# First inverse units behind the final spectral products, other loads held back, and 1/std in the transposes of the first layernorm

## The chip, the cores and the metric

The kernel runs on one core of one Trainium2 chip. Its engines work side by side: TensorE (PE in the profile, its weight loads PEld) multiplies matrices, VectorE (DVE), ScalarE (ACT) and GpSimd (POOL) work element by element, SyncE (SP) issues most transfers. Transfers run on 16 DMA engines. The metric is the device time of one execution in microseconds (us); less is better.

## What is computed

A conditioned block: a layernorm with scale and shift, a long convolution whose kernel comes from a diagonal state-space model, a gated residual, a second layernorm, a gated feed-forward part, a second residual. Sequence 2048, width 640, 128 states for each channel, hidden width 1728, all in float32.

```python
    mod = (_silu(c) @ w_mod).reshape(c.shape[0], 6, 1, -1)
    sa, ca, ga, sb, cb, gb = ...
    h = _layernorm(x, axis=-1) * (1 + ca) + sa
    x = x + ga * _A_ref(h, ...)      # S4D: K = 2 Re(C exp(A dt t)); y = irfft(rfft(u) rfft(K)) + u D
    h = _layernorm(x, axis=-1) * (1 + cb) + sb
    x = x + gb * _B_ref(h, ...)      # (silu(h w1) * (h w3)) w2
```

## The kernel before

**Two stages.** In the first, the convolution is computed for five groups of 128 channels (b = 0 to 4): the kernel's samples are generated, kernel and input go through a two-step Fourier transform on PE, the spectra are multiplied on DVE, and an inverse first step gives `zt`, which is stored to the DRAM buffer `zd`. In the second, the feed-forward part runs over four blocks of 512 rows (b = 0 to 3), each with 14 tiles of the hidden width (`ORDER`: 0, 13, 1 to 12; tile 13 is 64 wide, its gate and up halves in one matmul).

**The order of stage one** is made by a planner (`Plan`). Each task has an engine, an estimated cost, predecessors, buffers that it takes and gives, and a rank from a fixed table (`RANKS`). The planner simulates the tasks, and issues them in the order that comes out. `InOrder` fixes that order on every engine. A DMA task has a list of sizes from which the planner estimates its landing. So a changed predecessor or size may change the order of what comes after it.

**The final spectra** (`spectra_tasks` with b = 4). There are eight units i. For each, PE makes the spectrum of the input (`w4.i.f`, in the profile `fh`) and of the kernel (`w4.i.k`, `fk`), ACT holds the first (`w4.i.h`, `hz`), DVE multiplies in three steps (`w4.i.x0`, `x1`, `c`, `fp`). Every second unit completes a pair j, for which PE makes the inverse first step (`z4.j.z`, `fz`, 8 matmuls), two evictions follow (`z4.j.v0`, `v1`, into `zt`, three buffers), and two stores (`z4.j.o0`, `o1`, in the profile `zd<-zt`; the very last is `zd<-ztl` or `zd<-zt`). The planner's lines all carry the source line L157, that of the wrapper.

**Inverse units.** The second step of the inverse transform works on units of two row groups j: it loads a part of `zd` (`inverse_load`, 4 DMAs, `iz`), multiplies it with the constant `wd` on PE (`inverse`, `iy`), and DVE adds the result to the rows `x2`. Block 0 of the feed-forward part needs units 0 and 1. Their first 512 channels (groups 0 to 3 of stage one) are done inside the plan: tasks `iz0`, `iz1` (loads) and `ir0`, `ir1` (matmuls, additions, and the statistics `bn_stats` of these channels). The last 128 channels need the last stores; they are loaded behind the plan as `izb`, half from SP's queue and half from ACT's, and added in `self.inverse(0, 4, z, ps, ...)`. The last of these matmuls is `self.hold`: every DMA issued with `held_back` waits for it. Around them stand `awake` matmuls without a result. Units 2 to 7 run inside block 0 of the feed-forward part, in `mid`.

**The task `change`** closes the buffers of stage one and opens those of the feed-forward part. It loads `x2` of block 0 (4 DMAs) and `wd` (1 MB). `fw0` and `fw1` load the weights of the first two tiles of block 0 (`wr`, `w2r`), which ACT and POOL split into a high and a low part (`wh`, `wl`, `w2h`, `w2l`), as every operand of the feed-forward part is. All these transfers stand on SP's queue, which issues in order; the planner reckons with at most eight in flight.

**Layernorm of a block** (`ln2`): `bn_stats` per 128 channels, `bn_aggr` per row group, `rsqrt` (13 small operations on 128x4: an integer estimate and three Newton steps, then -mean/std), the normalised rows `xn` on ACT and DVE, PE transposes with the identity (`tp`), scale and shift by `cols` into `v`, and the split into `xh` and `xl`. For block 0 the 5 transposed tiles use the banks of `acc`.

**Feed-forward.** `up` makes gate and up (`gu`, three matmuls for each of 5 parts and each half: high by high, low by high, high by low); for the first two tiles of block 0 it runs jointly, part by part. `gate` makes `th`, `a`, `ah`, `al`; `down` adds to `acc`. The weights of a tile are asked for with `weights`, at the tile; their buffers are two deep. From `at(1000)` on, order is made by the framework's scheduler: program order by priority, where operands are ready. Its simulation lets a transfer go as soon as its buffer is free.

```python
        nxt = {0: self.ln2(0, pool, ps, self.stats, po)}
        self.at(2000)
        self.load_x2(1)

        def mid(b, m):
            if b == 0 and m in (1, 3):
                self.load_x2((m + 3) // 2)
            if b == 0 and 2 <= m + 1 < 8:
                self.inverse_unit(m + 1, ip, ps, "gu", 3)
```

Of the kernel before, what the change touches and what calls it, by code (L numbers as in the profile page):

```python
# [282 lines left out]
class K:  # L283
# [385 lines left out]
    def ln2(self, b, pool, ps, stats=None, po=None):  # L669

        nc = self.nc
        xs = self.x2[b]
        st, mv = stats or self.ln_begin(pool, f"n{b}")
        for j in range(4):
            self.ln_part(st, xs, j, KT - 1 if stats else 0, KT)
        rstd, nb = self.ln_end(pool, st, mv, f"n{b}")
        xn = pool.tile([P, 4, D], F32, name=f"xn{b}", tag="xn", bufs=1)
        for j in range(4):
            if j % 2:
                nc.vector.tensor_scalar(xn[:, j, :], xs[:, j, :], rstd[:, j:j + 1], nb[:, j:j + 1], op0=ALU.mult, op1=ALU.add)  # L680
            else:
                nc.scalar.activation(xn[:, j, :], xs[:, j, :], AF.Identity, scale=rstd[:, j:j + 1], bias=nb[:, j:j + 1])
        xh = pool.tile([P, KT, 512], F32R, name=f"xh{b}", tag="xh", bufs=2)
        xl = pool.tile([P, KT, 512], F32R, name=f"xl{b}", tag="xl", bufs=2)
        for k in range(KT):
            if po:
                pt = po.tile([P, 512], F32, name=f"tp{b}{k}", tag=f"acc{k}")
            else:
                pt = ps.tile([P, 512], F32, name=f"tp{b}{k}", tag="gu", bufs=3)
            for j in range(4):  # L690
                nc.tensor.transpose(pt[:, j * P:(j + 1) * P], xn[:, j, k * P:(k + 1) * P], self.ident)
# [11 lines left out]
    def weights_load(self, b, m, wp, ahead=False):  # L703

        nc = self.nc
        two = m < 13
        n = 2 if two else 1
        dma = (nc.gpsimd if ahead and POOLQ else nc.sync).dma_start
        raw = wp.tile([P, 2, KT, P], F32, name=f"wr{b}_{m}", tag="wr", bufs=2)
        f0 = m * P  # L710
        for i, src in enumerate((self.w1, self.w3)):
            if two:
                dma(raw[:, i], src[:, f0:f0 + P].rearrange("(k p) f -> p k f", p=P))
            else:
                dma(raw[:, 0, :, i * 64:(i + 1) * 64], src[:, f0:].rearrange("(k p) f -> p k f", p=P))
        w2r = wp.tile([P, D], F32, name=f"w2r{b}_{m}", tag="w2r", bufs=2)
        if two:
            dma(w2r, self.w2[m * P:(m + 1) * P, :])
        else:
            for i in range(2):  # L720
                dma(w2r[i * 64:(i + 1) * 64], self.w2[1664:1728, :])

        parts = []

        def high():
            wh = wp.tile([P, 2, KT, P], F32R, name=f"wh{b}_{m}", tag="wh", bufs=2)[:, :n]
            w2h = wp.tile([P, D], F32R, name=f"w2h{b}_{m}", tag="w2h", bufs=2)
            if b == 3:

                nc.vector.tensor_mul(w2r[:, :512], w2r[:, :512], self.gb)  # L730
            for i in range(n):
                self.nc.scalar.activation(wh[:, i], raw[:, i], AF.Copy)  # L732
# [22 lines left out]
    def ffn(self, nxt, wp, pool, ps, po, mid):  # L755

        pend = None
        for b in range(4):
            acc = None
            for i in range(14):  # L760
                m = self.ORDER[i]
                if b == 0 and i < 2:
                    if i == 0:
                        w = [self.ahead.pop((0, x)) for x in range(2)]
                        both = self.up(0, [(self.ORDER[x], *w[x][:2]) for x in range(2)], *nxt[0], ps)
                    w2h, w2l = w[i][2:]
                    gu = both[i]
                else:
                    wh, wl, w2h, w2l = self.ahead.pop((b, i), None) or self.weights(b, m, wp)
                    gu, = self.up(b, [(m, wh, wl)], *nxt[b], ps)  # L770
                if pend is not None:
                    self.down(*pend)
                    if i == 0:
                        self.output(b - 1, pend[1], pool, ps)
                if acc is None:
                    acc = [po.tile([P, 512], F32, name=f"acc{b}{k}", tag=f"acc{k}") for k in range(KT)]
                ah, al = self.gate(b, m, gu, pool)
                pend = (m, acc, ah, al, w2h, w2l)
# [79 lines left out]
    def run(self):  # L858
# [48 lines left out]
        def change():  # L907
            close("gw", "tbl", "gp", "early")
            self.xp, self.ip, self.wp = open_("xp"), open_("ip"), open_("wp")
            self.wd = self.xp.tile([P, NJ, 2, 64], F32, name="wd")  # L910
            self.x2 = [self.xp.tile([P, 4, D], F32, name="x20")]
            nc.sync.behind = nc.tensor.prev
            self.load_x2(0)
            nc.sync.dma_start(self.wd, self.t_wd)
            nc.sync.behind = None
            self.stats = self.ln_begin(self.ip, "n0")
        add = plan.add
        add("change", None, 0, change, [f"g{b}.7.p", f"g{b}.7.d"] + [f"h{b}.{i}.x" for i in range(4)], 0)
        add("fx", "SP", 0, None, ["change"], 0, dma=[327680] * 4 + [1048576])
        self.ahead = {}  # L920
        split = {}
        cut = b * P
# [5 lines left out]
            add(f"fs{m}", "POOL", 5.0, lambda m=m: self.ahead.__setitem__((0, m), split[m][1](self.nc.gpsimd)), [f"fa{m}"], W + 30)  # L928

        def load_w(m):  # L930
            q = nc.gpsimd if POOLQ else nc.sync
# [9 lines left out]
            for j in (2 * u, 2 * u + 1):  # L941
                self.ln_part(self.stats[0], self.x2[0], j, 0, KT - 1)
        for u in range(2):
            add(f"iz{u}", "SP", 0, lambda u=u: load_z(u), ["change", "fx"] + [f"z{b - 1}.{j}.o{f}" for j in range(4) for f in range(2)], W, dma=[262144] * 4)
            add(f"ir{u}", "PE", 2.4, lambda u=u: first_rows(u), [f"iz{u}"] + [f"{x}{b}.{i}.e" for x in ("hh", "k") for i in range(8)], W + 25)
        plan.run()
        self.nc = real
        self.at(1000)
# [5 lines left out]
        ps = open_("ps", space=PSUM)  # L954
        self.x2 += [pool.tile([P, 4, D], F32, name=f"x2{b}") for b in range(1, 4)]
        z = self.inverse_load("izb", ip, "izb", 1, 0, 4, cut, D, real.scalar)
        self.awake(nc.tensor, po.tile([P, 512], F32, name="awake0", tag="acc4"), 8)
        self.hold = nc.tensor.prev = self.inverse(0, 4, z, ps, "gu", 3, cut, D)
        self.awake(nc.tensor, po.tile([P, 512], F32, name="awake1", tag="acc4"), 3)
        nxt = {0: self.ln2(0, pool, ps, self.stats, po)}  # L960
        self.at(2000)
        self.load_x2(1)

        def mid(b, m):
            if b == 0 and m in (1, 3):
                self.load_x2((m + 3) // 2)
            if b == 0 and 2 <= m + 1 < 8:
                self.inverse_unit(m + 1, ip, ps, "gu", 3)
            if b == 0 and m == 9:
                self.gb_row(pool, ps)  # L970
            if m == 8 and b < 3:
# [385 lines left out]
    def early_tasks(self, e):  # L1357
# [133 lines left out]
        add("cols", "ACT", .9, lambda: self.mod_cols(pm[1]), ["mc4"], W["col"], take=[("f2", 1), ("hz", 1)])  # L1491
        add("colsf", None, 0, None, ["cols"], give=[("f2", "cols"), ("hz", "cols")])

    def gb_row(self, pool, ps):

        pr = ps.tile([P, 512], F32, name="prg", tag="gu", bufs=3)
# [64 lines left out]
```

## Time and profile before

| | |
|---|---|
| runs | 998.25 us median of 3 (996.02 to 1000.65) |
| the profiled execution | 998.14 us, span from first to last instruction 996.4 us |
| granted TensorE clock, mean | 0.975 |
| PE busy | 893.9 us, 90% of the span |
| DVE / ACT / POOL busy | 665.9 / 496.8 / 287.7 us |
| DMA | 122.03 MB, mean 122 GB/s |
| stage one | up to about 384 us |
| feed-forward part | first up matmul at 398.52 us, to the end |

A page of the profile and the queries of its trace give: windows (busy time of each engine in a stretch), the chain of waits (the work that ended last, followed back from step to step), the timeline (instructions in order of time: start, length, engine, line, operation, output and inputs, count, and in brackets the idle time before and what ended it), groups (instructions of one line and shape: busy us, mean ns), DMA issues (sizes, and time from issue to landing). Lengths of PE instructions overlap: the time of a row of matmuls is read from start to start.

### The profile page before, as it was taken

Reading aid. Unit: us, or ns where it says so; the run is one execution under the profiler, and the core shown is the slowest. Engines: PE = TensorE matmul, PEld = TensorE weight load, DVE = VectorE, ACT = ScalarE, POOL = GpSimd, SP = SyncE. Lnnn points to the kernel's source line nnn. Section 1 sums busy time; section 2 is a strip of 40 time slices with the busy share of each in tenths; the row PEclk is TensorE's granted clock in tenths of the full one; section 3 lists DMA queues with packets and bytes.
Section 4 is the critical chain, followed back from the end, with each engine's and each line's share of the span. In section 5 each row is a group of like instructions: output and inputs, shape, how many; then the busy total and the mean of one; then the engine's idle time right before and its main releaser. Section 6 shows DMA issues by size and latency. Waiting matters only on the chain.

```text
span 996.4 us, 20192 instructions
## 1 busy us (share of the span) xinstructions
PE 893.9 (90%) x8095; PEld 708.2 (71%) x8095; DVE 665.9 (67%) x1234; ACT 496.8 (50%) x829; POOL 287.7 (29%) x293
## 2 busy tenths in 40 slices
PE   1464777889999997999999999999999999999997
PEld 1133666767788863667788888888888888888885
DVE  7998999999999674677564553463644544645443
ACT  6878787979788731432243332342432332433221
POOL 1798798989898330100000000000000000000000
PEclk9986998999999999999999999999999999999999
DMA  9955553615041297997232363332443323542301
GB/s 215 266 177 188 123 132 99 156 45 129 24 108 46 73 266 206 221 236 173 61 98 73 106 166 92 86 100 79 118 134 107 92 80 94 145 119 80 106 27 53
DMA packets 141189, 122.03 MB, mean 122 GB/s; under 512 B 13480, under 2 KB 124840, under 8 KB 139688
## 3 DMA queue, kind: packets, MB, share of 16 engines
q1 hardware_dynamic: 140360, 119.84, 45.6%
q8 instruction: 63, 1.03, 0.5%
q10 hardware_dynamic: 736, 0.92, 0.3%
q14 instruction: 30, 0.25, 0.1%
HBM read 99.75 MB, written 20.97 MB: 121 GB/s over the span
## 4 chain that ended last, share of the span: by engine, by line
PE 72%; DVE 13%; DMA 5%; ACT 4%; issue 3%; POOL 1%; SPq 1%; ACTq 0%; DVEq 0%; POOLq 0%
PE acc L833 19%; PE gu L798 13%; PE gu L797 12%; PE gu L796 12%; PE ps L157 4%; DVE yy L157 3%; DMA xs<-in_x 3%; PE kps L157 2%; PE fk L157 2%; PE fz L157 2%; DVE fp L157 2%; DMA zd<-zt 2%; PE fh L157 2%; DVE hn L157 2%; DVE xx L157 2%
## 5 line engine op out<-in xcount | busy, mean ns | idle before, releaser
L798 PE MATMUL gu<-xh,wl 128*128 128x512 f32 x540 | 213.1, 395 | 0.0
L797 PE MATMUL gu<-xl,wh 128*128 128x512 f32 x540 | 211.8, 392 | 0.0
L796 PE MATMUL gu<-xh,wh 128*128 128x512 f32 x540 | 210.7, 392 | 0.7 <-ACT xh L666 0.7
L732 ACT ACTIVATE wh<-wr 128x640 fp32r<-128x640 f32 x105 | 71.9, 732 | 135.6 <-PE gu L797 129.3
L744 POOL MEMSET w2l<- 64x640 f32 x3 | 1.9, 630 | 451.0 <-PE acc L833 451.0
L797 PEld LDWEIGHTS gu<-xl,wh 128*128 128x128 f32 x540 | 101.6, 188 | 23.6 <-DVE xl L667 0.2
L796 PEld LDWEIGHTS gu<-xh,wh 128*128 128x128 f32 x540 | 101.4, 188 | 23.2 <-ACT xh L666 1.0
L798 PEld LDWEIGHTS gu<-xh,wl 128*128 128x128 f32 x540 | 101.6, 188 | 21.3
L809 ACT ACTIVATE th<-gu 128x512 f32<-128x512 f32 x52 | 31.1, 598 | 127.7 <-PE gu L798 127.5
L811 DVE TENSOR_TENSOR a<-a,gu 128x512 f32<-128x512 f32 x52 | 35.8, 688 | 86.2 <-PE gu L798 85.9
L157 POOL TENSOR_TENSOR yy<-e,e 128x512 f32<-128x512 f32 x80 | 86.3, 1094 | 17.9 <-PE kps L157 11.8
L833 PE MATMUL acc<-w2h,ah 128*128 128x512 f32 x220 | 87.1, 396 | 0.0
L833 PE MATMUL acc<-w2l,ah 128*128 128x512 f32 x220 | 87.1, 396 | 0.0
L733 ACT ACTIVATE w2h<-w2r 128x640 fp32r<-128x640 f32 x54 | 39.9, 738 | 94.6 <-issue 53.0
L810 DVE SCALAR_TENSOR_TENSOR a<-th,gu 128x512 f32<-128x512 f32 x52 | 35.7, 687 | 76.1 <-ACT th L809 76.0
L745 DVE TENSOR_TENSOR w2l<-w2r,w2h 128x640 fp32r<-128x640 f32 (+1 forms) x54 | 44.4, 822 | 58.0 <-ACT w2h L733 57.9
L741 DVE TENSOR_TENSOR wl<-wr,wh 128x640 fp32r<-128x640 f32 x105 | 82.4, 819 | 0.0
L157 POOL TENSOR_TENSOR ph<-p,p 128x1024 int32<-128x1024 int32 x40 | 79.9, 1997 | 5.2 <-ACT tr L157 4.5
L833 PE MATMUL acc<-w2h,al 128*128 128x512 f32 x204 | 77.6, 396 | 0.0
L157 DVE TENSOR_TENSOR yy<-yy,tr 128x512 f32<-128x512 f32 (+1 forms) x80 | 75.5, 946 | 0.9 <-ACT tr L157 0.6
L157 PE MATMUL kps<-yy,xx 128*32 128x64 f32 x2560 | 52.7, 239 | 24.9 <-DVE xx L157 21.9
L157 PEld LDWEIGHTS kps<-yy,xx 128*32 128x32 f32 x2560 | 46.1, 119 | 34.5 <-issue 17.5
(231 smaller groups left out, 1694.7 us busy)
## 6 DMA issues: line engine op xcount, KB each, us to landing
wr<-in_w SPq DMA_DIRECT2D x104, 320.0 KB, 3.9
w2r<-in_w SPq DMA_DIRECT2D x52, 320.0 KB, 3.0
zd<-zt SPq DMA_DIRECT2D x39, 256.0 KB, 2.7
iz<-zd SPq DMA_DIRECT2D x24, 320.0 KB, 9.2
xs<-in_x SPq DMA_DIRECT2D x16, 320.0 KB, 11.2
hs<-hb SPq DMA_DIRECT2D x20, 256.0 KB, 2.4
xb<-hs SPq DMA_DIRECT2D x20, 256.0 KB, 4.5
x<-in_x SPq DMA_DIRECT2D x16, 320.0 KB, 9.8
```

The lines of the kernel that those rows point to most:

```text
L157: self.prev = self.k.order(f(*a, **kw), self.prev)
L732: self.nc.scalar.activation(wh[:, i], raw[:, i], AF.Copy)
L733: self.nc.scalar.activation(w2h, w2r, AF.Copy)
L741: eng.tensor_tensor(wl[:, i], raw[:, i], wh[:, i].bitcast(F32), op=ALU.subtract)
L745: eng.tensor_tensor(w2l[q], w2r[q], w2h[q].bitcast(F32), op=ALU.subtract)
L796: nc.tensor.matmul(pg, wh[:, k, :], xh[:, k, :], start=(k == 0), stop=False)
L797: nc.tensor.matmul(pg, wh[:, k, :], xl[:, k, :], start=False, stop=False)
L798: nc.tensor.matmul(pg, wl[:, k, :], xh[:, k, :], start=False, stop=(k == KT - 1))
L809: nc.scalar.activation(th, gu[0], AF.Tanh, scale=0.5)
L810: nc.vector.scalar_tensor_tensor(a, th, 1.0, gu[0], op0=ALU.add, op1=ALU.mult)
L811: nc.vector.tensor_mul(a, a, gu[1])
L833: nc.tensor.matmul(acc[k], *two(a, w), start=(m == 0 and i == 0), stop=(m == 12 and i == 2))
```

## The change

1. **Units 0 and 1 in the plan.** `iz{u}` (the loads) now also follow the evictions `z4.u.v0`, `z4.u.v1`. `ir{u}` (the matmuls, additions and statistics) now also follow `z4.3.z`, the last `fz`. The sizes by which the planner estimates the loads become two of 512 KB in place of four of 256 KB; the DMAs themselves are the same four.
2. **`wd`.** `change` loads only the first quarter of it (256 KB); the rest is loaded with `held_back`, behind `x2` of block 1.
3. **Weights.** All loads of `weights_load` go by `held_back`. The two that are issued inside the plan are not touched, since `hold` isn't set there. The third tile's are issued once after the layernorm of block 0, ahead of `x2` of block 1; the fourth's and later ones at their tiles, as before in program order, but not before `hold`.
4. **Units 2 to 7** run in `mid` of tile u instead of u - 1.
5. **`awake`** ahead of the `izb` products: 3 calls in place of 8.
6. **Layernorm of block 0.** `xn` becomes mean - x, on ACT for all four row groups, each behind its own `bn_aggr`. `rsqrt_short` has 9 small operations. Four DVE operations make diagonals `dg` from the identity and the result. The 20 transposes become 20 f32 matmuls with `xn` stationary and `dg` moving, so that the transposed rows come out scaled by 1/std. Blocks 1 to 3 keep `ln_end` and the transposes.

```diff
+        if po:
+            dg = pool.tile([P, 4, P], F32, name="dg", bufs=1)
+            for j in range(4):
+                nc.vector.bn_aggr(mv[:, j, :], st[:, j, :, :])
+                nc.scalar.activation(xn[:, j, :], xs[:, j, :], AF.Identity, scale=-1.0, bias=mv[:, j, 0:1])
+            y = self.rsqrt_short(pool, mv[:, :, 1], 4)
+            for j in range(4):
+                nc.vector.tensor_scalar(dg[:, j, :], self.ident, y[:, j:j + 1], -0.375, op0=ALU.mult, op1=ALU.mult)
...
-                nc.tensor.transpose(pt[:, j * P:(j + 1) * P], xn[:, j, k * P:(k + 1) * P], self.ident)
+                if po:
+                    nc.tensor.matmul(pt[:, j * P:(j + 1) * P], xn[:, j, k * P:(k + 1) * P], dg[:, j, :], start=True, stop=True)
+                else:
+                    nc.tensor.transpose(pt[:, j * P:(j + 1) * P], xn[:, j, k * P:(k + 1) * P], self.ident)
...
-        dma = (nc.gpsimd if ahead and POOLQ else nc.sync).dma_start
+        def dma(to, src):
+            self.held_back(nc.sync.dma_start(to, src))
...
-                    wh, wl, w2h, w2l = self.ahead.pop((b, i), None) or self.weights(b, m, wp)
+                    wh, wl, w2h, w2l = self.third() if (b, i) == (0, 2) else self.weights(b, m, wp)
...
-            nc.sync.dma_start(self.wd, self.t_wd)
+            nc.sync.dma_start(self.wd[:, :4], self.t_wd[:, :4])
...
-        add("fx", "SP", 0, None, ["change"], 0, dma=[327680] * 4 + [1048576])
+        add("fx", "SP", 0, None, ["change"], 0, dma=[327680] * 4 + [262144])
...
-            add(f"iz{u}", "SP", 0, lambda u=u: load_z(u), ["change", "fx"] + [f"z{b - 1}.{j}.o{f}" for j in range(4) for f in range(2)], W, dma=[262144] * 4)
-            add(f"ir{u}", "PE", 2.4, lambda u=u: first_rows(u), [f"iz{u}"] + [f"{x}{b}.{i}.e" for x in ("hh", "k") for i in range(8)], W + 25)
+            add(f"iz{u}", "SP", 0, lambda u=u: load_z(u), ["change", "fx"] + [f"z{b - 1}.{j}.o{f}" for j in range(4) for f in range(2)] + [f"z{b}.{u}.v{f}" for f in range(2)], W, dma=[524288] * 2)
+            add(f"ir{u}", "PE", 2.4, lambda u=u: first_rows(u), [f"iz{u}", f"z{b}.3.z"] + [f"{x}{b}.{i}.e" for x in ("hh", "k") for i in range(8)], W + 25)
...
-        self.awake(nc.tensor, po.tile([P, 512], F32, name="awake0", tag="acc4"), 8)
+        self.awake(nc.tensor, po.tile([P, 512], F32, name="awake0", tag="acc4"), 3)
...
         self.at(2000)
+        self.third = self.weights_load(0, self.ORDER[2], wp)
         self.load_x2(1)
+        self.held_back(nc.sync.dma_start(self.wd[:, 4:], self.t_wd[:, 4:]))
...
-            if b == 0 and 2 <= m + 1 < 8:
-                self.inverse_unit(m + 1, ip, ps, "gu", 3)
+            if b == 0 and 2 <= m < 8:
+                self.inverse_unit(m, ip, ps, "gu", 3)
...
+    def rsqrt_short(self, pool, var, n):
+        V = self.nc.vector
+        v, w, h, q = (pool.tile([P, n], F32, name=f"rq_{x}", bufs=1) for x in "vwhq")
+        V.tensor_scalar(v, var, 1.0, EPS, op0=ALU.mult, op1=ALU.add)
+        V.tensor_scalar(w.bitcast(I32), v.bitcast(I32), -0.5, float(0x5F3759DF), op0=ALU.mult, op1=ALU.add)
+        V.tensor_mul(h, v, w)
+        V.scalar_tensor_tensor(h, h, -0.5, w, op0=ALU.mult, op1=ALU.mult)
+        V.scalar_tensor_tensor(w, h, 1.5, w, op0=ALU.add, op1=ALU.mult)
+        V.tensor_mul(h, v, w)
+        V.tensor_mul(h, h, w)
+        V.scalar_tensor_tensor(q, h, -10.0 / 3, h, op0=ALU.add, op1=ALU.mult)
+        V.scalar_tensor_tensor(q, q, 5.0, w, op0=ALU.add, op1=ALU.mult)
+        return q
```

More of the change, by code (lines that the diff above doesn't have):

```diff
@@ L675, in ln2 @@
             self.ln_part(st, xs, j, KT - 1 if stats else 0, KT)
-        rstd, nb = self.ln_end(pool, st, mv, f"n{b}")
+        dg = None
         xn = pool.tile([P, 4, D], F32, name=f"xn{b}", tag="xn", bufs=1)
[L678 to L682, printed above, removed]
+        if po:
[7 more added lines that the diff above has]
+        else:
+            rstd, nb = self.ln_end(pool, st, mv, f"n{b}")
+            for j in range(4):
+                if j % 2:
+                    nc.vector.tensor_scalar(xn[:, j, :], xs[:, j, :], rstd[:, j:j + 1], nb[:, j:j + 1], op0=ALU.mult, op1=ALU.add)
+                else:
+                    nc.scalar.activation(xn[:, j, :], xs[:, j, :], AF.Identity, scale=rstd[:, j:j + 1], bias=nb[:, j:j + 1])
         xh = pool.tile([P, KT, 512], F32R, name=f"xh{b}", tag="xh", bufs=2)
@@ L690, in ln2 @@
             for j in range(4):
-                nc.tensor.transpose(pt[:, j * P:(j + 1) * P], xn[:, j, k * P:(k + 1) * P], self.ident)
+                if po:
+                    nc.tensor.matmul(pt[:, j * P:(j + 1) * P], xn[:, j, k * P:(k + 1) * P], dg[:, j, :], start=True, stop=True)
+                else:
+                    nc.tensor.transpose(pt[:, j * P:(j + 1) * P], xn[:, j, k * P:(k + 1) * P], self.ident)
             v = pool.tile([P, 512], F32, name=f"v{b}{k}", tag="v", bufs=3)
@@ L930, in load_w @@
         def load_w(m):
-            q = nc.gpsimd if POOLQ else nc.sync
+            q = nc.sync
             q.behind = nc.tensor.prev
```

## The prediction

> **What bounds the kernel now.** I looked first at the page for the busy shares, then at the stretch where the convolution hands over to the feed-forward part: the windows, the chain of waits, the timeline of each engine, the DMA queue. Columns of the windows: stretch, length, busy us and instructions of PE, PEld, DVE, ACT and POOL, then granted clock, DMA share, GB/s.
>
> ```profile
> 345.00:384.10 39.10, 36.65 (x360) 24.42 (x357) 23.79 (x55) 13.03 (x22) 8.24 (x6) 0.96 1.01 261
> 363.57:366.98 3.41, 1.36 (x14) 0.57 (x10) 2.94 (x7) 1.67 (x3) 3.37 (x3) 1.00 1.10 275
> 366.98:370.40 3.42, 3.35 (x11) 1.66 (x11) 0.69 (x1) 0.60 (x1) 2.16 (x2) 0.50 1.10 290
> 392.00:450.00 58.00, 53.81 (x248) 38.09 (x247) 40.32 (x107) 22.90 (x34) 2.59 (x2) 1.00 1.04 227
> ```
>
> From 345 to 384 and again from 392 to 450 the DMA engines are full. In the window at 363.6 PE sits idle for 2 us, and in the next it runs at half clock. The chain of waits (start, length, what) through this place:
>
> ```profile
> 363.66 6.04 DMA zd<-zt
> 369.76 8.34 DMA zd<-zt
> 378.19 0.61 ACT zt L157
> 378.81 5.28 DMA zd<-zt
> 384.11 0.67 ACTq L642
> 384.81 3.81 DMA izb<-zd
> 391.39 0.30 DVE mv_n L350
> 394.41 0.93 ACT xn L682
> 395.38 1.76 PE tp L691 x14
> 398.52 0.97 PE gu L796 x3
> ...
> 543.75 3.49 PE acc L833 x15
> ```
>
> So between 363.7 and 384.1 the end is set by stores of `zd`, each slow because the queue is full, and by the buffers `zt` that these stores give back. Behind the last store come its reload `izb`, the layernorm, and the first up matmul at 398.52. After that PE sets the pace (the last row: 15 matmuls back to back, 0.23 us each).
>
> **The seam: inverse units moved, loads held.** PE and DVE there, by the timeline:
>
> ```profile
> 363.13 1.07 PE L157 MATMUL fk<-sp,wb 128*64 128x128 f32 x16
> 364.51 0.68 DVE L157 TENSOR_TENSOR fp<-fk,hz 128x512 f32<-128x512 f32 x1
> 365.83 0.75 DVE L157 TENSOR_TENSOR fp<-fp,fk 128x256 f32<-128x256 f32 x2
> 366.25 4.09 PE L157 MATMUL iy<-iz,wd 128*64 128x512 f32 x7 [2.05 <-DMA iz<-zd]
> 374.94 2.29 PE L157 MATMUL fz<-fp,wz 64*128 64x512 f32 x8 [0.34 <-DVE fp L157]
> 377.15 1.94 PE L157 MATMUL iy<-iz,wd 128*64 128x512 f32 x8
> 379.56 6.60 PE L157 MATMUL awake<-wd,ident 128*128 128x512 f32 x15
> ```
>
> Unit 0 (`iy` at 366.25) stands in PE's order ahead of the last spectral unit. It waits 2.05 us for its load and blocks PE for 4.09 more; the last `fh` and `fk` come behind it, and the last `fz` only at 374.94. With both units behind the last `fz`, unit 7's `fh` and `fk` follow the `fk` that ends at 364.20: 2 x 1.07 gives 366.34. DVE needs 2.07 us a unit (364.51 to 366.58), and ends this one at 368.7. The last `fz` then runs from 368.9 for 2.29 us to 371.2 instead of 377.2, its last eviction (0.61) ends at 371.8, and the last store is issued at 371.9 instead of 378.81. If the `fz` of pair 2 slips in between, this is up to 2.3 us later, which the longest flight below stands for.
>
> The store's flight: the loads that filled the queue are gone.
>
> ```profile
> 367.48 1.09 SPq L713 DMA_DIRECT2D wr<-in_w  x2
> 370.83 4.42 SPq L713 DMA_DIRECT2D wr<-in_w  x2
> 375.34 0.84 SPq L718 DMA_DIRECT2D w2r<-in_w  x1
> wd<-in_t_wd SPq DMA_DIRECT2D x1, 1024.0 KB, 10.1
> DMA to landing us min/median/max: 2.3/4.0/5.6
> ```
>
> The last row is the flight of the `zt` stores, 2.3 to 5.6 us. I take 3.3, under the median, since only unit 1's load is still draining. The last store lands at 371.9 + 3.3 = 375.2 instead of 384.09 (378.81 + 5.28): **8.9 us** earlier; by the bounds 6.6 (5.6 us flight) to 9.9 (2.3 us). The queue must be able to follow: six weight loads of 327,680 bytes (1.97 MB) and three quarters of `wd` (0.79 MB) leave this stretch, 2.75 MB, at 261 GB/s 10.5 us. So the queue allows the same, and neither bound undercuts the other. On SP the two loads of 4 DMAs each now stand behind the first stores of pairs 0 and 1, which lets `zt` go earlier; the later stores stand behind the loads, whose data land before PE reaches the units at 371.2.
>
> What must stay covered: units 0 and 1 now run at the very end, 2 x 1.94 us of PE, to 375.1. Their DVE work is 4 additions and 16 statistics:
>
> ```profile
> L157 DVE TENSOR_TENSOR x<-iy,x 128x512 f32<-128x512 f32 x4 | 2.8, 692 | 6.3 <-PE iy L157 6.2
> L157 DVE BATCH_NORM_STATS2 st_n<-x 128x6 f32<-128x128 f32 x16 | 3.3, 278 | 0.0
> ```
>
> 6.1 us, from 371.8 to 377.9, hidden by the last store's flight and the reload, which (4.5 us from issue to landing, 384.11 to 388.62) ends at 379.7. Cover gone, as with a load of unit 1 that lands 2 us later than I have it, each further us counts in full. The keep-awake matmuls take 0.44 us each, two to a call: 3 calls end at 377.7; 8 would have ended at 382.1, on the path. PE then idles some 2 us. The rows above show half clock after a window busy for 1.36 of 3.41 us; the same here would cost up to 1.7 us. The Trainium skill (TensorE: Matmul & The Clock Gate, What's actually happening) has the clock fall only after at least one idle window of about 3.4 us; here 2 us of idle were enough, so the measurement decides, and by the page alone this cost would be nothing.
>
> **Layernorm of the first block.**
>
> ```profile
> 390.62 0.58 DVE L350 BATCH_NORM_AGGREGATE mv_n<-st_n 128x2 f32<-128x30 f32 x3
> 391.77 0.17 DVE L325 TENSOR_SCALAR rs_v_n<-mv_n 128x4 f32<-128x4 f32 x1
> 394.15 0.16 DVE L337 SCALAR_TENSOR_TENSOR rs_n_n<-mv_n,rs_y_n 128x4 f32<-128x4 f32 x1
> 394.41 1.73 ACT L682 ACTIVATE xn<-x,rs_n_n,rs_y_n 128x640 f32<-128x640 f32 x2 [15.63 <-DVE rs_n_n L337]
> 395.30:397.90 2.60, 2.40 (x20) 2.17 (x20) 1.00 1.04 221
> 514.90:516.20 1.30, 1.05 (x8) 1.00 (x8) 1.00 0.00 0
> ```
>
> Call A the end of the last aggregate, 391.69. Before: 13 small operations, 0.2 us apart (391.77 to 394.15), `xn`, first transpose at A+3.7, 20 of them in 2.4 us, first up matmul at A+6.8. After: 9 small operations take 1.8 us, to A+1.9; four diagonals of 128x128 (no such operation here; between the 0.17 us of the 128x4 row and the 0.28 us of the 128x128 statistics, I take 0.2, nearest in size) are there from A+2.1 to A+2.7. The four centred `xn` on ACT (1.73 for two, so 0.82 apart) start behind the first aggregate, about 391.0, and end at A+2.7: hidden by the diagonals. PE starts at A+2.15 and no longer transposes but multiplies. The last two rows are PE's 20 transposes, and the four plain f32 products of the same 128x128 shape of `gb_row`, which stand as 8 records: 1.05 us / 8 = 0.13 a record with its tail, 0.11 without. Twenty products are 40 records, 4.5 us, so PE is through at A+6.7 and the first up matmul, whose `xh` is long ready, follows there: **-0.1 us**. Bounds: -0.6 (0.11 a record, no wait for the fourth `xn`) to +1.0 (0.13 and a late fourth).
>
> The Trainium skill (TensorE: Matmul & The Clock Gate, Terms) calls the transpose mode "4× faster for FP32"; the rows make it 2.2 (0.26 for two records against 0.12).
>
> **What the held loads cost later.** All 2.75 MB now wait for the last `izb` product, at 390.03 - 8.9 = 381.1, where SP starts the next loads.
>
> ```profile
> 390.03 3.79 SPq L632 DMA_DIRECT2D x<-in_x  x8
> 393.86 11.31 SPq L642 DMA_DIRECT2D iz<-zd  x8
> 411.97 10.59 SPq L713 DMA_DIRECT2D wr<-in_w  x4
> 408.31 2.62 ACT L732 ACTIVATE wh<-wr 128x640 fp32r<-128x640 f32 x4
> 412.73 2.59 PE acc L833 x10
> ```
>
> In the order of the program stand the weights of the third tile (0.98 MB), `x2` of block 1 (1.31), the rest of `wd` (0.79), `x2` of block 2 (1.31), unit 2 (1.31), the weights of the fourth tile (0.98): 6.7 MB, at 227 GB/s 29.4 us and 2 us to the first byte, landed at 412.5. Up to here PE has, from 389.5, the joint up product of 45 matmuls (at 0.23 us, 10.3), a gap of about 2.4 for `th` to `ah` (3.9 before, from 398.52 + 10.3 to 412.73, partly filled with unit 2, which now comes a tile later), `down` 3.5, up 6.9, the narrow `down` 2.3: the fourth tile is due at 414.9. That is just enough. The fifth stands behind 3.6 MB more, 428.4, and is due at 427.7; from there each tile moves 2.3 MB, 10.1 us, against 12.8 of PE. I charge **+1.0 us**. Bounds: -1.3 (two `wh` conversions instead of four stand ahead of `ah` on ACT, 2.62 / 2) to +5 (a tenth less bandwidth over 10.3 MB).
>
> **The sum** is made against the profiled execution, 998.14 us (its span of 996.4 and 1.7 around it), 0.1 us under the median 998.25 of the runs: 998.14 - 8.9 - 0.1 + 1.0 = **990.1 us**. Its own range: the good bounds together, -9.9, -0.6 and -1.3, give 986.3; -6.6 with +1.0 and +3 of the loads 995.5.
>
> **Rivals.**
> 1. *Starved first block, slower.* If SP issues as it did (8 `x`, 8 `iz`, more `x`, then `wr` at 411.97), `x2` of block 3 and unit 3 (2.6 MB, 11.5 us) get ahead of the fourth tile's weights: landed at 424, PE waits 10.7 us, and the idle window halves the clock, 1.7: 998.14 - 8.9 - 0.1 + 1.0 + 10.7 + 1.7 = 1002.5. For it: the saturated windows, and that the rows show `wr` last. Against it: those were later tiles; the fourth tile's stand ahead in the program. It decides once those weights land more than 9 us after 414.9.
> 2. *The order on SP keeps the stores back.* The change does only half of what it says: stores of pairs 2 and 3 sit behind the load of unit 1 in a queue still full, the last one leaves 3 us later and flies 5.6: 998.14 - 3.9 - 0.1 + 1.0 = 995.1. For it: 1.01 DMA share; against it: 2.75 MB less.
> 3. *Dear products.* Four times a transpose, 20 x 0.12 x 4 = 9.6 us, puts the first up matmul at A+11.75, 4.9 us later than now: 998.14 - 8.9 + 4.9 + 1.0 = 995.1. The `gb_row` record speaks against it. This is the factor of the skill's page named above.
>
> **The chances.** The forecast 0.75, starved 0.12, stores 0.08, products 0.05. A difference under 0.5% (5 us, faster under 993.3, slower over 1003.2) can't be told from none. Of the forecast 0.70 lies below 993.3 and 0.05 above; rivals 2 and 3 are no change; of the starved case 0.05 is no change and 0.07 slower. Faster 0.70, same 0.23, slower 0.07. The range 986.5 to 996.0 holds the forecast but its edge (0.04) and rivals 2 and 3; it leaves out the starved case.
>
> **What would show it.** The last `fz` ends near 371 with the clock at 1.00 throughout, the last `zd` store lands at 375 (right) or past 379 (rival 2); `iy` of both units follows; aggregates to first up matmul 6.7 us, PE's 40 records about 4.5 (rival 3: 9.6); PE without waits for `wr` in the first block, `wh` of the fourth tile near 411 (rival 1: near 424). If DVE still works on the units' statistics when `izb` lands, or blocks 1 to 3 are not as long as before, the reasoning is wrong.

## The result and the profile after

The changed kernel takes **1011.91 us** (median of 4 runs, 1011.55 to 1013.72), the kernel before, run beside it, 997.70 us (4 runs, 996.02 to 1000.65). The ratio is 1.0137, with a 95% interval of 1.0120 to 1.0154: **slower**, by 1.4%. The prediction was 990.1 us, with 996.0 as its upper end. It was wrong.

The profiled execution took 1011.79 us, its span is 1010.0. Three marks divide the span: the first up matmul, the first transpose of block 1, and the end.

| stretch, us | before | after | difference |
|---|---|---|---|
| start to the first up matmul | 398.52 | 391.32 | -7.2 |
| block 0, up to the first transpose of block 1 | 103.99 | 118.13 | +14.1 |
| blocks 1 to 3 and the end | 493.9 | 500.5 | +6.7 |
| span | 996.4 | 1010.0 | +13.6 |

So the seam gave about what it should, and two later places took back three times as much. PE, SP and DVE at the seam, by the timeline of the changed kernel (start, length, engine, line, what, count, idle before):

```profile
367.66 4.73 PE L157 MATMUL fz<-fp,wz 64*128 64x512 f32 x16
372.32 3.65 PE L157 MATMUL iy<-iz,wd 128*64 128x512 f32 x16
377.78 2.84 PE L157 MATMUL awake<-wd,ident 128*128 128x512 f32 x6 [1.81 <-DVE x L157]
373.58 0.42 SPq L157 DMA_DIRECT2D zd<-zt  x1
376.87 1.25 SPq L642 DMA_DIRECT2D izb<-zd  x2
384.02 0.29 DVE L682 BATCH_NORM_AGGREGATE mv_n<-st_n 128x2 f32<-128x30 f32 x1
386.13 0.87 DVE L686 TENSOR_SCALAR dg<-ident,rq_q 128x128 f32<-128x128 f32 x4
386.57 4.70 PE L703 MATMUL tp<-dg,xn 128*128 128x128 f32 x40 [1.17 <-DVE dg L686]
391.32 0.97 PE L811 MATMUL gu<-xh,wh 128*128 128x512 f32 x3
```

The last `fz` ends at 372.4 (377.2 before), the last store leaves at 373.58 (378.81) and its reload at 376.87 (384.1). The 40 records of the new products take 4.70 us. The chain of waits (start, length, what) goes another way here than through the reload:

```profile
376.54 1.20 DVE x L157 x2
377.78 2.84 PE awake L157 x6
380.62 2.02 PE iy L652 x16
```

The `awake` matmuls waited 1.81 us for the additions of the two units on DVE, and the products of the reload start right behind them. The reload left from 376.87 to 377.6 and was 2.9 to 3.6 us on its way, so its data came between 379.7 and 381.1, about when `awake` was through.

Then the first block. ACT's timeline, PE's one row where it stops and the row where it goes on, and the chain of waits (start, length, what):

```profile
400.78 0.60 ACT L824 ACTIVATE th<-gu 128x512 f32<-128x512 f32 x1 [4.14 <-PE gu L813]
401.30 1.37 ACT L747 ACTIVATE wh<-wr 128x640 fp32r<-128x640 f32 x2
411.88 0.74 ACT L747 ACTIVATE wh<-wr 128x640 fp32r<-128x640 f32 x1 [9.21 <-DMA wr<-in_w]
412.64 0.59 ACT L830 ACTIVATE th<-gu 64x512 f32<-64x512 f32 x1
...
414.07 0.74 ACT L747 ACTIVATE wh<-wr 128x640 fp32r<-128x640 f32 x1 [0.36 <-DMA wr<-in_w]
414.71 0.61 ACT L666 ACTIVATE ah<-a 128x512 fp32r<-128x512 f32 x1
...
427.89 1.42 ACT L747 ACTIVATE wh<-wr 128x640 fp32r<-128x640 f32 x2 [9.58 <-DMA wr<-in_w]
429.21 0.61 ACT L666 ACTIVATE ah<-a 128x512 fp32r<-128x512 f32 x1
```

```profile
409.38 0.40 PE L813 MATMUL gu<-xh,wl 128*128 128x512 f32 x1
415.38 0.80 PE L848 MATMUL acc<-ah,w2h 128*128 128x512 f32 x1 [5.60 <-ACT ah L666]
```

```profile
387.38 13.45 DMA x<-in_x
400.85 13.20 DMA wr<-in_w
417.50 10.02 DMA wr<-in_w
430.51 2.40 PE acc L848 x5
```

In ACT's queue the conversions `wh` of the fourth tile stand ahead of `ah` of the first tile. They wait 9.21 us for `wr`, and `ah`, whose input `a` was done on DVE at 403.5, waits behind them. PE's first `down` needs this `ah`: PE is through with all up products that it can do at 409.8 and idles 5.60 us. With the fifth tile it happens again, 9.58 us on ACT and, by the trace's starts and ends, 4.7 on PE.

Before, `ah` stood behind four conversions too, but these had their weights, and it came 13.5 us after the first up matmul (398.52):

```profile
412.05 0.63 ACT L666 ACTIVATE ah<-a 128x512 fp32r<-128x512 f32 x1
```

After the change, on SP, `x2` of block 2 and the load of unit 2 left ahead of the fourth tile's weights:

```profile
386.76 4.42 SPq L632 DMA_DIRECT2D x<-in_x  x4
392.26 6.51 SPq L642 DMA_DIRECT2D iz<-zd  x4
399.51 1.73 SPq L723 DMA_DIRECT2D wr<-in_w  x2
```

What idle time does to the clock, by windows (stretch, length, busy us of PE, PEld, DVE, ACT, POOL, clock, DMA share, GB/s):

```profile
391.32:509.45 118.13, 107.77 (x466) 76.83 (x467) 69.48 (x189) 33.42 (x52) 2.58 (x2) 0.96 0.71 171
410.16:413.58 3.42, 0.00 (x0) 0.00 (x0) 0.83 (x1) 1.68 (x3) 0.00 (x0) 1.00 1.12 254
413.58:416.99 3.41, 1.61 (x4) 1.32 (x5) 2.81 (x4) 1.87 (x4) 0.00 (x0) 0.50 0.99 205
416.99:420.41 3.42, 3.42 (x10) 2.65 (x9) 2.06 (x3) 1.25 (x2) 0.00 (x0) 0.50 1.00 237
423.82:427.24 3.42, 2.03 (x10) 0.95 (x8) 0.00 (x0) 0.00 (x0) 0.00 (x0) 1.00 0.95 230
427.24:430.65 3.41, 0.14 (x1) 0.14 (x2) 1.99 (x4) 2.76 (x5) 0.00 (x0) 1.00 0.25 74
430.65:434.06 3.41, 3.41 (x9) 1.54 (x9) 3.41 (x10) 0.43 (x1) 0.00 (x0) 0.50 0.80 207
```

Three windows of 3.41 us run at half clock; PE is busy in 8.4 us of them, and half of that, 4.2, is lost. Before, the same block had its PE busy for 103.16 of 103.99 us, at full clock:

```profile
398.52:502.51 103.99, 103.16 (x466) 74.83 (x467) 70.96 (x191) 34.27 (x53) 2.59 (x2) 1.00 0.74 170
```

Blocks 1 to 3 have no waits in either kernel. There the chain shows one row for each tile's `down`, so the distance of two rows is the period of a tile (30 up and 15 down matmuls). Before, then after:

```profile
533.38 3.49 PE acc L833 x15
543.75 3.49 PE acc L833 x15
```

```profile
540.76 3.50 PE acc L848 x15
551.29 3.50 PE acc L848 x15
```

10.37 us became 10.53 (551.29 - 540.76). The 39 full tiles of these blocks by 0.16 give 6.2 of the 6.7 us. From start to start, by the trace, neighbouring up matmuls stand 234.4 ns apart in place of 229.9, the down matmuls 234.1 in place of 232.7 (means; how long a gap still counts as back to back moves them all by up to 0.5 ns). The code there is the same.

### The profile page after: what moved, and what is told of

Read it like the earlier page. It is cut to its first block, busy times and chain, and to the rows that moved or that the text cites. A ratio compares the mean times of both kernels' runs of the same rounds, so it can differ in the third digit from the quotient of the medians.

```text
span 1010.0 us, 20218 instructions
## 1 busy us (share of the span) xinstructions
PE 901.1 (89%) x8105; PEld 710.5 (70%) x8105; DVE 666.3 (66%) x1233; ACT 497.2 (49%) x830; POOL 286.7 (28%) x293
## 4 chain that ended last, share of the span: by engine, by line
PE 72%; DVE 14%; DMA 5%; ACT 4%; issue 3%; SPq 1%; POOL 1%; DVEq 0%; ACTq 0%
PE acc L848 18%; PE gu L811 12%; PE gu L813 12%; PE gu L812 12%; PE ps L157 4%; DVE yy L157 3%; PE fz L157 3%; PE fk L157 2%; PE kps L157 2%; DMA wr<-in_w 2%; PE fh L157 2%; DVE fp L157 2%; DVE xx L157 2%; PE iy L652 2%; DVE hn L157 1%
## 5 line engine op out<-in xcount | busy, mean ns | idle before, releaser
L811 PE MATMUL gu<-xh,wh 128*128 128x512 f32 x540 | 214.2, 398 | 0.1
```

What stands on the lines that cost most here:

```text
L811: nc.tensor.matmul(pg, wh[:, k, :], xh[:, k, :], start=(k == 0), stop=False)
```

## The experiments

Two theories were to be tested, with their rivals. **Queue**: in block 0, late weights hold up conversions, and what stands behind these holds up PE; the rival is bandwidth alone. **Place**: the small tiles `rs_*` of `ln_end` used to be allocated by block 0, ahead of `xh`; now block 1 allocates them, behind it. So `xh`, `xl`, `v`, `th`, `a`, `ah`, `al` and `u` begin 160 bytes lower (`xh` at 154944 in place of 155104 in each partition), and matmuls that read from there are slower; the rival is that the later start or the other order does it.

The remainder is that of the start of `xh` by 512 bytes; the two paces are means from start to start in blocks 1 to 3. Idle PE is the length of block 0 less PE's busy time in it. Runs of one group shared their chip and the runs of the kernel before; the other columns are from one profiled execution of each kernel.

| kernel | remainder | up, down ns | block 0 us | idle PE there | us, ratio to before, interval |
|---|---|---|---|---|---|
| before | 480 | 229.9, 232.7 | 104.0 | 0.8 | |
| after | 320 | 234.4, 234.1 | 118.1 | 10.4 | 1011.91, 1.0137 (1.0120 to 1.0154) |
| e1_shift | 288 | 233.0, 232.2 | 121.5 | 14.0 | 1009.34, 1.0110 (1.0084 to 1.0137) |
| e2_before_shift | 448 | 233.6, 233.2 | 104.4 | 0.8 | 1003.44, 1.0051 (1.0020 to 1.0082) |
| e3_order | 320 | 234.4, 234.1 | 114.4 | 8.8 | 1008.21, 1.0104 (1.0077 to 1.0130) |
| e4_early | 320 | 234.4, 234.1 | 109.1 | 3.9 | 1009.49, 1.0122 (1.0096 to 1.0149) |
| e5_place | 480 | 230.4, 232.7 | 117.3 | 10.4 | 1005.06, 1.0069 (1.0044 to 1.0094) |
| e6_spread | 320 | 234.4, 234.1 | 105.9* | 6.9 | 1007.59, 1.0086 (1.0060 to 1.0111) |
| e7_both | 480 | 230.4, 232.7 | 105.6* | 7.7 | 1001.10, 1.0021 (1.0004 to 1.0038) |
| e8_place_x | 480 | 229.6, 233.0 | 117.7 | 11.3 | 1004.28, 1.0062 (1.0041 to 1.0083) |
| e9_all | 480 | 230.5, 232.7 | 95.5* | 0.1 | 992.03, 0.9930 (0.9914 to 0.9946) |
| e10_x2_late | 480 | 230.4, 232.7 | 103.9 | 1.3 | 990.22, 0.9918 (0.9896 to 0.9940) |
| e11_ln | 480 | 230.5, 232.8 | 107.8 | 3.0 | 998.45, 0.9996 (0.9983 to 1.0010) |
| e12_x512 | 0 | 233.7, 233.4 | 105.2 | 1.3 | 996.10, 0.9970 (0.9957 to 0.9982) |

(*: here some units stand behind the first transpose of block 1, which makes block 0 shorter and what follows longer.)

### The place of the tiles

**e1_shift and e2_before_shift**: 32 bytes of padding, in the changed kernel and in the one before.

```diff
-        u = pool.tile([P, 512], F32, name=f"u{b}", tag="u", bufs=1)
+        u = pool.tile([P, 520], F32, name=f"u{b}", tag="u", bufs=1)[:, :512]
```

> The changed kernel with one tile made 32 bytes longer, so that every tile of the feed-forward pool that lies before it, xh and xl among them, starts 32 bytes lower. In the kernel before they start at 32 beyond a multiple of 64 bytes, in the changed one on a multiple. Theory placement: the 1620 up matmuls of the changed kernel stand 0.234 us apart instead of 0.230 because of where their moving operand starts; the shift brings 0.230 back and 7 us of time, 1005 us. Rival: the slower pace has another cause (transfers, the clock); 1012 us, 0.234.

> The kernel before with the same 32 bytes, so that xh and xl come to lie on a multiple of 64. Theory placement: 0.234 us and 7 us slower, 1005 us. Rival: 998 us, 0.230.

In the kernel before, the padding alone, with the order of work unchanged, moves the up matmuls from 229.9 to 233.6 ns and makes the kernel 0.5% slower (1.0051): a place costs some 5 us by itself. A tile's period, by the chain:

```profile
535.53 3.50 PE acc L833 x15
546.02 3.50 PE acc L833 x15
```

That is 10.49 us. In the changed kernel the same padding puts `xh` 32 bytes past a multiple of 64, as in the kernel before; 230 ns were expected, and it came from 234.4 to 233.0 only. So a rule by multiples of 64 bytes is wrong.

**e5_place**: the 160 bytes given back, so that `xh` and everything behind it lie where they lay before.

```diff
-        v, w, h, q = (pool.tile([P, n], F32, name=f"rq_{x}", bufs=1) for x in "vwhq")
+        v, w, h, q, r = (pool.tile([P, n], F32, name=f"rq_{x}", tag=f"rs_{x}") for x in "vwynt")
...
-        V.scalar_tensor_tensor(q, q, 5.0, w, op0=ALU.add, op1=ALU.mult)
+        V.scalar_tensor_tensor(r, q, 5.0, w, op0=ALU.add, op1=ALU.mult)
```

> The changed kernel with xh and every tile behind it back at the addresses they had before the change (the small reciprocal-root tiles of the first block share the five small tiles that the later blocks use, so 160 bytes are moved). Nothing else is different. Placement theory: the up matmuls of blocks 1 to 3 stand 229.9 ns apart again instead of 234.4, and from the first transpose of block 1 to the end it takes 493.9 us instead of 500.5; the whole 1011.9 - 6.7 = 1005.2 us. Rival (the pace is set by what the change does to the order of work or to the first block): 234 ns apart, 500.5, and 1011.9 us in all.

1005.06 us where 1005.2 was expected. Its chain has the old period, 548.43 - 538.07 = 10.36 us:

```profile
538.07 3.49 PE acc L848 x15
548.43 3.48 PE acc L848 x15
```

Block 0 hardly moves (118.1 to 117.3, PE idle for 10.4 us as in the change): the two losses are separate.

**e8_place_x and e12_x512**: of what PE reads, only `xh` and `xl` moved, by padding each of the three buffers of `v`; in e12_x512 (552 in place of 584) on top of e10_x2_late, below.

```diff
-            v = pool.tile([P, 512], F32, name=f"v{b}{k}", tag="v", bufs=3)
+            v = pool.tile([P, 584], F32, name=f"v{b}{k}", tag="v", bufs=3)[:, :512]
```

> The changed kernel with xh and xl alone moved, to the same remainder of 512 bytes that they had before the change (480 instead of 320); th, a, ah, al and u stay where the change put them. If the place of the moving operand sets the pace of the up matmuls: they stand 229.9 ns apart, the down matmuls (moving w2h, untouched) stay at 234, and 1215 up matmuls of blocks 1 to 3 by 4.5 ns give 5.5 us: 495 from block 1 to the end, 1006.4 in all. If it is the place of what ACT and DVE write beside PE (th, a, ah, al): 234 and 500.5, 1011.9 in all.

> The kernel with x2 of blocks 2 and 3 loaded late and the places restored (990.2 us), with xh and xl alone 480 bytes lower, so that both begin at a multiple of 512 bytes; all that ACT and DVE write beside them stays. It asks which places are the quick ones. So far the up matmuls stood 229.6 to 230.5 ns apart where xh began 480 bytes past a multiple of 512, and 233.0 to 234.4 where it began 288, 320 or 448 past. If even starts are quick and only odd ones cost: 226 to 230 ns, and 985 to 990 us. If 480 is a place of its own, by its distance to other tiles: 233 to 234.5, and 990.2 + 5 = 995.

e8_place_x puts `xh` and `xl` back to the remainder 480 and leaves `th`, `a`, `ah` and `al` at 320; the up matmuls come down to 229.6 ns. So for the up matmuls it is the place of the moving operand that counts, not what ACT and DVE write. The down matmuls were to stay at 234, since 12 of 15 have `w2h` or `w2l` moving, which lie at the same address in every kernel here; they came to 233.0. What moves them between 232.2 and 234.1 in the table isn't shown. e12_x512 is against the guess that even starts are quick: at a multiple of 512 it is 233.7 ns, and 5.1 us more from block 1 to the end (499.6 against 494.5) than e10_x2_late. Of the five remainders tried (0, 288, 320, 448, 480) only 480 is quick. Why, stays open.

### The first block

**e3_order**: on ACT and DVE the conversions of the fourth to seventh tile (m = 2 to 5) stand behind `ah` and `al` of the tile two earlier in `ORDER`; loads as in the change.

```diff
+    def behind(self, e, ins, b, m):
+        if b == 0 and 2 <= m < 6:
+            self.order(ins, self.gated[m - 1][e])
...
-                self.nc.scalar.activation(wh[:, i], raw[:, i], AF.Copy)
+                self.behind(0, self.nc.scalar.activation(wh[:, i], raw[:, i], AF.Copy), b, m)
```

> The changed kernel with one more rule of order: in block 0 the conversions wh, w2h and wl of the third to sixth tile stand on ACT and DVE behind the gate of the tile two places earlier. No transfer is changed. Theory queue: what costs is not that the weights of the fourth tile come late, but that ah of the first tile stands behind their wh on ACT; PE's two idle stretches of 5.6 and 4.7 us and the half clock behind them go, 11 to 15 us, about 999 us. Rival bandwidth: PE needs those weights itself at the same time; it idles as before, 1009 to 1012 us.

1008.21 us where 999 was expected: a miss. Block 0 takes 114.4 in place of 118.1 us. The first wait is gone (`ah` of the first tile starts at 403.12), and one of the same kind has come up on DVE:

```profile
427.60 0.82 DVE L760 TENSOR_TENSOR wl<-wr,wh 128x640 fp32r<-128x640 f32 x1 [9.94 <-ACT wh L751]
429.35 0.88 DVE L655 TENSOR_TENSOR x<-iy,x 128x320 f32<-128x320 f32 x2
```

```profile
429.89 1.34 PE L652 MATMUL iy<-iz,wd 128*64 128x320 f32 x4 [8.66 <-DVE x L655]
```

The addition of the inverse unit stands behind the low part `wl`, which waits for the late weights, and PE waits for the addition's bank. So while these loads came late, another place in the queue only changed who stood behind them.

**e4_early**: the change, but its weights not held back.

```diff
-            self.held_back(nc.sync.dma_start(to, src))
+            nc.sync.dma_start(to, src)
```

> The changed kernel with the weights of the third tile and later ones not held back, so that those of the third and fourth tile are again issued among the stores of the last spectra. Theory queue: the wait of wh and the two idle stretches go (12 to 15 us gained), and the first up matmul comes 4 to 7 us later, by 1.97 MB at 261 GB/s: about 1004 us. Rival, held loads bring nothing at the seam since PE sets its pace: the first up matmul stays where it is, 998 us. Rival bandwidth: 1010 us.

1009.49 us where 1004 was expected. Block 0 loses 9 us of its length (109.1), but the first up matmul comes at 402.67, 11.3 later than in the change and 4.2 later than before, though the last `fz` ends at 374.6. The profile is of the slowest of four runs, 1013.95 us; if the other runs lost their 4.5 us ahead of the first up matmul, it came near 398 there, as before the change (an estimate). In the chain stands now a unit's load, 6.56 us in a queue full of weights, and behind it its products:

```profile
375.89 6.56 DMA iz<-zd
382.59 3.66 PE iy L157 x6
```

So the seam's gain hangs on the held loads; the moved units alone don't bring it.

**e6_spread and e7_both**: weights of the fourth tile ahead of `x2` of block 1, units 2 to 7 at every second tile, `x2` of blocks 2 and 3 later in the program; e7_both with the places of e5_place.

```diff
-        self.third = self.weights_load(0, self.ORDER[2], wp)
+        self.early = {i: self.weights_load(0, self.ORDER[i], wp) for i in (2, 3)}
...
-            if b == 0 and m in (1, 3):
-                self.load_x2((m + 3) // 2)
-            if b == 0 and 2 <= m < 8:
-                self.inverse_unit(m, ip, ps, "gu", 3)
+            if b == 0 and m in (6, 9):
+                self.load_x2(m // 3)
+            if b == 0 and m in (3, 5, 7, 9, 11, 12):
+                self.inverse_unit((3, 5, 7, 9, 11, 12).index(m) + 2, ip, ps, "gu", 3)
```

> The changed kernel, with its loads still held, but the weights of the fourth tile loaded right behind those of the third, ahead of x2 of block 1; units 2 to 7 stand behind tiles 4, 6, 8, 10, 12 and 13 of the first block instead of 3 to 8; x2 of blocks 2 and 3 is loaded five tiles later. Theory (weights that come late hold up the conversions, and what stands behind these on ACT and DVE holds up PE): the first block, from the first up matmul to the first transpose of block 1, takes 104 to 106 us instead of 118.1, PE idles less than 2 us there and runs at half clock less than 4; in all 1011.9 - 13 = 999 us. Rival (the 2.75 MB taken from the stretch before must be paid anywhere in the first block): PE idles as long at another place, 114 us or more, in all 1008 or more. Pace of the up matmuls unchanged, 234 ns.

> Both of the former edits in one kernel. If the two losses are separate and add up: 1011.9 - 6.7 - 13 = 992 us, 0.6% faster than before, with 104 to 106 us for the first block and 493.9 from block 1 to the end. If the pace of the up matmuls is tied to the starved first block (a later start, a clock that doesn't recover), or the loads collide again, 999 or more.

Both miss, by about 9 us. The losses add up as expected (e6 to e7: 6.5 us for the places), and the wait for the fourth tile is gone, but the one for the fifth has stayed, with 6.6 us on PE in place of 4.7 (ACT in e6_spread):

```profile
425.87 1.53 ACT L747 ACTIVATE wh<-wr 128x640 fp32r<-128x640 f32 x2 [17.28 <-DMA wr<-in_w]
427.31 0.61 ACT L666 ACTIVATE ah<-a 128x512 fp32r<-128x512 f32 x1
```

SP's order in e7_both shows why: all 8 DMAs of `x2` of blocks 2 and 3 still left between 403.6 and 413, ahead of the fifth tile's `wr` at 414.4. A place in the program doesn't hold a transfer whose buffer is free.

**e10_x2_late and e9_all**: the places of e5_place, and `x2` of blocks 2 and 3 held by a real dependency, on the products of units 2 and 4. In e10_x2_late this is all; e9_all is e7_both with each unit's load and these `x2` held by the unit before. The cut is from e10_x2_late.

```diff
-            if b == 0 and m in (1, 3):
-                self.load_x2((m + 3) // 2)
             if b == 0 and 2 <= m < 8:
-                self.inverse_unit(m, ip, ps, "gu", 3)
+                mm = self.inverse_unit(m, ip, ps, "gu", 3)
+                if m in (2, 4):
+                    first, self.hold = self.hold, mm
+                    self.load_x2(m // 2 + 1)
+                    self.hold = first
```

> The changed kernel with the places of xh restored, and of its loads only x2 of block 2 and x2 of block 3 moved: they wait for the products of units 2 and 4. Units stay at tiles 3 to 8 as in the change. This is the edit to its first block that leaves most alone. Theory (1.3 MB less ahead of the fourth tile's weights, 2.6 less ahead of the fifth's: at 227 GB/s landed 5.8 and 11.5 us earlier): gu0 to the first transpose of block 1 takes 107 us instead of 117.3, PE idles under 3 us, 1005.1 - 10 = 995. Rival (order on ACT and DVE alone, wherever the loads stand): 115 or more, and 1003.

> The kernel of both former edits (places of xh restored, weights of the fourth tile first, units spread), and now each unit's load waits for the products of the unit before it, and x2 of blocks 2 and 3 for units 3 and 5, so that 2.6 MB of x2 and 1.3 MB of unit 3 no longer stand ahead of the fifth tile's weights. Theory (what is left of the loss in the first block is those weights, landing at 426 to 428 where ACT needs them by 419): they land by 412, PE idles less than 1 us there and never runs at half clock, and of 1001.1 us the 7.6 of idle time and half of the 6.8 at half clock go: 990 us, 0.8% faster than before. Rival (the first block is bound by the sum of its bytes): a wait comes up at a later tile of the block, 997 or more.

Both beat the kernel before: 990.22 us (0.9918, 0.9896 to 0.9940) and 992.03. The first is 5 us better than expected; 3 of these are block 0, 103.9 us where 107 were expected. SP, ACT, PE and the window of block 0 in e10_x2_late:

```profile
392.79 1.95 SPq L723 DMA_DIRECT2D wr<-in_w  x2
```

```profile
404.83 0.74 ACT L747 ACTIVATE wh<-wr 128x640 fp32r<-128x640 f32 x1 [2.65 <-DMA wr<-in_w]
406.22 0.74 ACT L747 ACTIVATE wh<-wr 128x640 fp32r<-128x640 f32 x1 [0.65 <-DMA wr<-in_w]
408.08 0.63 ACT L666 ACTIVATE ah<-a 128x512 fp32r<-128x512 f32 x1
```

```profile
418.30 0.50 PE L848 MATMUL acc<-ah,w2h 128*128 128x512 f32 x1 [1.21 <-ACT w2h L748]
391.03:494.94 103.91, 102.57 (x466) 74.46 (x467) 69.44 (x189) 33.34 (x52) 2.58 (x2) 1.00 0.83 196
```

The queue order on ACT is still the bad one (`wh` ahead of `ah`), but the weights leave and land 7 us earlier (392.79 against 399.51, 404.83 against 411.88), `ah` comes in time, PE idles 1.3 us in the whole block and the clock stays full. From e5_place to e10_x2_late block 0 shrinks by 13.4 us: 9.1 of idle time, and 4.4 for the half clock (8.8 us of PE's work in e5_place ran at it). The two differ by the order of the loads alone, not by their bytes, so the rival, bandwidth alone, is refuted.

**e11_ln**: the kernel before, with the layernorm's part of the change alone and the places kept.

> The kernel before with the layernorm's part of the change alone, and xh and all behind it at the addresses they had. Prediction's term: from the end of the last aggregate to the first up matmul 6.7 us, with 7.0 seen in the changed kernel, against 6.83 before: no difference that can be measured, 998.4 within 1.5. Rival (the layernorm part carries some of the loss into the blocks, through its 40 f32 products or the f32 diagonals): 1001 or more.

998.45 us, ratio 0.9996 (0.9983 to 1.0010): nothing that can be measured. Its row in the table is from the slowest of twelve runs, 1003.09 us, so its block 0 of 107.8 us may not be typical.

## Why the prediction was wrong

- **The seam, -8.9 us: right, but for one step.** By the profiled pair it is 7.2. Stage one ran 1.2 us late in that execution (a row of `fh` at 348.38 in place of 347.16), which leaves 8.4. Ten executions with held loads have their first up matmul between 388.2 and 391.3 (mean 390.2), three of kernels without them at 398.5, 398.9 and 399.8 (mean 399.1): 8.9 apart, the layernorm in it. The last `fz` was forecast for 371.2 and came at 372.4, the reload for 375.2 and left at 376.87; both are off by about that late start. The step that differs: 3 calls of `awake` were to end at 377.7, with some 2 us of idle PE behind them. They waited for DVE and ended at 380.6, with the 1.81 idle us ahead of them, about when the reload landed. That this cost little is luck. The idle time cost no half clock.
- **The layernorm, -0.1 us: right.** A + 6.7 was forecast and 384.31 + 7.0 measured, against 6.83 before: +0.2, inside the bounds. The 40 records took 4.70 us (4.5). Rival 3 is refuted by that row.
- **The order on SP, rival 2: refuted.** The last store left at 373.58 and its reload at 376.87. (Its sum, too, is off: 3 us later and 5.6 in flight leave 3.6 of the 8.9, not 3.9, and give 995.4.)
- **The held loads, +1.0 us: here the argument failed.** The landings were right: 412.5 forecast for the fourth tile's weights, 411.88 and 414.07 the starts of its conversions; 428.4 for the fifth, 427.89 that of its. The due time was wrong. The text took the weights as due when PE multiplies with them, "the fourth tile is due at 414.9", and called 412.5 "just enough". But the first to need them is ACT, and behind it in ACT's queue stands `ah` of the first tile. From the first up matmul to `ah` it took 13.5 us before (398.52 to 412.05); with the same distance `ah` was due at 404.9, ahead of any landing, and it came at 414.71. The bound of -1.3 even counted two conversions ahead of `ah`, as time, and not as a wait that they carry. Four conversions stood ahead of it, as before. The block cost +14.1, beyond the bound of +5: about 9.5 more idle time and 4.2 at half clock.
- **Rival 1, the starved first block, 1002.5: the right direction, at 0.12, with the wrong point of decision.** It asked for weights later than 414.9 + 9; they landed before 414.9, and PE starved all the same. `x2` of block 3 and unit 3, which it put ahead of the fourth tile's weights, left SP at 404.06 and 409.03, behind them (399.51). What e10_x2_late took from ahead of them is `x2` of block 2, which stands in the forecast's own list. The rival's sum has a slip: 424 less 414.9 is 9.1 and not 10.7, which makes it 1000.9.
- **What was missing: the places, +6.7 us.** The text said that blocks 1 to 3 had to be as long as before, and never asked what a tile taken away does to the addresses of the others. e5_place gives 6.9 us back by addresses alone.
- The sum of -7.2, +14.1 and +6.7 is the 13.6 us by which the span grew. With both losses undone, e10_x2_late stands at 990.22 us: the seam and the layernorm are worth what was forecast.

## What to carry to other kernels

A load that is delayed is due when the first engine in order reaches an instruction that waits for it, not when its data are multiplied; so read each queue for what stands behind that instruction, and who waits for it. To keep a transfer back, give it a dependency: a later place in the program doesn't hold it if its buffer is free. And when a change adds or drops small tiles, compare the start addresses of the big operands before and after.

## What the hardware showed

- **The place of a moving operand** sets the pace of the up matmuls (128x512, back to back): 229.6 to 230.5 ns where `xh` and `xl` begin 480 bytes past a multiple of 512, 233.0 to 234.4 at 0, 288, 320 and 448 (that 512 is the right measure isn't shown). The Trainium skill (SBUF — State Buffer, Operand start alignment) asks only for a start at a multiple of the element size; every place here meets that, and up to 2% of the pace still differs.
- **The clock** changes at edges of a 3.41 us grid. In the first block after the change, the windows in which PE was busy for 0.00 and 0.14 us were each followed by half clock, the one with 2.03 was not, and 1.61 us of work at half clock were not enough to get back. Counted over the clock records of all 14 traces, every full-clock window with less than 1.38 us of work was followed by half clock (98 of 98), and none of 3365 with 2.5 or more. At half clock, none of 101 windows with less than 2.5 us of work led back to full clock, and all of 106 with more than 2.81 did. In between it went both ways. The Trainium skill (TensorE: Matmul & The Clock Gate, What's actually happening) has half clock after at least one idle window of about 3.4 us and full clock after a busy one. The two states and the grid agree, but idle doesn't mean without work: the prediction's row of before has half clock behind a window busy for 1.36 us.
